# Gated linear attention and a mixture of experts on one core: old state scaled on GpSimd, later weight loads, last tile in one operation, a new order

## The chip, the cores and the metric

The kernel runs on one core of a Trainium2 chip. The metric is the device time of one execution in microseconds (us). The kernel before takes 383.08 us (median of three runs, 382.61 to 383.10).

The engines are named as the profile names them: PE (TensorE matmul) and PEld (its weight loads), DVE (VectorE), ACT (ScalarE), POOL (GpSimd), SP (the engine that issues most DMAs). Each works through its own queue in order.

## The reference

Two parts follow one another. The first is a gated linear attention over 4 batches, 8 heads, 768 tokens and 48 channels per head:

```python
for t in range(S):
    state = alpha[:, :, t, :, None] * state + np.einsum('bhd,bhe->bhde', k[:, :, t], v[:, :, t])
    y[:, :, t] = np.einsum('bhd,bhde->bhe', q[:, :, t], state)
```

Its output, 3072 tokens of 384 channels, goes into a mixture of 8 experts. Each token takes its own best expert, or, where its local gate is at 0.5 or more, the expert of the token before it in its batch. The output row is `p[e] * (relu(x @ w1[e]) @ w2[e])` with hidden size 1024, and `p` the softmax of the 8 logits.

## The kernel before, in words

**Attention.** The tokens are cut into 24 blocks of 128 tokens. Block i belongs to batch i % 4, so the states of four batches (tiles `st`) are carried side by side. A block's inputs come in by three DMAs into one of four slots `x0` to `x3` (slot i % 4): k, q (112x512 each) and the gates a (112x521). The values come by two more DMAs (`vt`, three buffers).

A block goes through these steps. ACT writes a separator into the gates (`mid`, "ACT x<-P 112x4"). DVE scans the gates backwards in two halves into `sf` and forwards into `A`. POOL multiplies k by `sf` and q by `A` in place ("x<-x,sf", "x<-x,A"). PE transposes k ("cs,x 112x112") and multiplies k with q in 64x64 pieces ("x 64x64"). DVE masks that product into `pq`. PE multiplies `pq` with `vt`, and the transposed keys `kk` with `vt`, which updates the state on DVE. PE then adds q times the state ("st,x") to the block's output. ACT copies the output to `XR`, SP stores it to `xd` in DRAM, PE transposes it ("cs,XR") and multiplies it with the gate weights (`logits`).

**The old state.** From the fifth block on, `carry` (line 549) scales the state that the batch had before (part 2 of `s3`) by the total decay of the block, column 0 of each head pair's stretch in `sf`, into part 0 of `s3`. Four ACT operations of 112x48 do it, one for each head pair.

**Routing and experts.** After blocks 8, 16, 20 and 24, `route` finds each token's expert and its place in that expert's list. One expert (number 0) is worked on in two parts, 0a for the first 256 tokens of its list and 0b for the rest. The 0a part starts while the last groups are still being routed. Experts are matmuls in three passes: each weight and each activation is split into a high and a low half (`w1h`, `w1l`, `w2h`, `w2l`, `xh`, `xl`, `hh`). The high half is a cast on ACT; the low half is a subtraction, on POOL for w1 and on DVE for w2. Expert 0's weights come in seven pieces (three of w1 with 512 KB, four of w2 with 384 KB) through four `raw` buffers; the blocks behind whose mask (`marks`) each piece is loaded stand in `WAT`. An output tile is scaled by the token's probability from PSUM into `yo` and scattered to DRAM by an indirect DMA on POOL. The last tile of all (96 rows) is scaled in two halves, one on DVE and one on ACT (lines 1145 to 1150).

**The order.** Nothing is issued where it stands in the code. `add` hands every step to a planner as a task with an engine, a cost, a priority (mostly the block number plus an offset), and what it reads and writes. `Plan.order` runs through the tasks with these costs, takes on each engine the ready task of lowest priority, and writes the queues out in that order. `SHIFT` moves the priority of a kind of task, by engine and by the name that it writes; `ROUTE` and `DUE` move the routing and the early expert; `SLACK`, `TAIL`, `PAGE_US` are the planner's costs of a hand-over, of a DMA's landing and of fetching PE instructions. Where the plan leaves PE idle for a while before the experts start, it puts in filler matmuls ("P<-dz 128x240", results unused); `MARG`, `WINDOW` and `SHARE` decide where and how many. Twenty fillers stand at the start in any case (`WARM`).

## Time and profile before

| | us |
|---|---|
| median of three runs | 383.08 (382.61 to 383.10) |
| profiled execution, its own time | 382.43 |
| its span, first to last instruction | 380.5 |
| PE busy in the span | 367.9 (97%) |
| DVE, ACT, POOL busy in the span | 224.7, 199.3, 203.2 |
| granted TensorE clock, mean | 0.998 |

The page divides the span into 40 slices and gives for each engine the share that it was busy, for PE also the clock that was granted. Busy times of PE are modelled for pipelined matmuls, so that one instruction's end lies behind the start of the next. Fillers count as PE work. In the answers, "idle before" is the time that an engine stood still ahead of a group, with what ended it behind the arrow. 1.93 us of the execution's 382.43 us lie outside the span.

### The profile page before, as it was taken

The numbers are of one execution on the slowest core, as the hardware profiler recorded it, in microseconds if no ns is written. First come the engines' busy times: TensorE is split into PE (matmuls) and PEld (weight loads), VectorE is DVE, ScalarE is ACT, GpSimd is POOL, SyncE is SP. The second block draws the span as 40 slices with busy tenths as digits, with TensorE's granted clock in tenths as the row PEclk, the third lists the DMA queues.
The fourth block names the chain that finished last, engine by engine and source line by source line (L and its number), as shares of the span: only waits on it lengthen the run. The fifth ranks groups of instructions, "written<-read, shape, count | busy, mean of one in ns | idle before, by whom it ended". The sixth has DMA issues, their size and how long they took to land. (4 is left out here: it accounts for less than half of the span.)

```text
span 380.5 us, 10980 instructions
## 1 busy us (share of the span) xinstructions
PE 367.9 (97%) x4151; PEld 342.2 (90%) x4151; DVE 224.7 (59%) x554; ACT 199.3 (52%) x576; POOL 203.2 (53%) x293
## 2 busy tenths in 40 slices
PE   7999999999899999999999999999999999999993
PEld 7988888888788898998899999999999899999993
DVE  5998969878896486455516434642761763543310
ACT  2397687799596573646505523541660672532300
POOL 7765375787547047888624832842663574432012
PEclk9999999999999999999999999999999999999999
DMA  8999999989972255557425622741652552421000
GB/s 217 254 265 262 270 254 258 280 239 261 269 218 75 66 208 161 184 157 249 144 79 180 202 70 65 245 132 43 215 158 83 177 193 62 136 84 43 17 22 28
DMA packets 28665, 62.08 MB, mean 163 GB/s; under 512 B 4660, under 2 KB 11023, under 8 KB 28611
## 3 DMA queue, kind: packets, MB, share of 16 engines
q1 hardware_dynamic: 24576, 51.23, 45.9%
q0 software_dynamic: 3488, 9.86, 7.9%
q8 instruction: 33, 0.54, 0.6%
q10 hardware_dynamic: 546, 0.28, 0.3%
q14 instruction: 22, 0.17, 0.2%
HBM read 51.91 MB, written 9.86 MB: 162 GB/s over the span
## 5 line engine op out<-in xcount | busy, mean ns | idle before, releaser
L329 PE MATMUL P<-w2h,hh_mp 128*128 128x384 f32 (+3 forms) x376 | 100.0, 340 | 0.0
L329 POOL TENSOR_TENSOR w1l<-raw,w1h 128x256 fp32r<-128x256 f32 x96 | 69.6, 750 | 27.9 <-ACT w1h L329 21.0
L329 POOL DMA_INDIRECT out<-yo_mp,li_mp x25 | 26.6, 1063 | 88.8 <-DVE yo_mp L329 71.5
L329 ACT CAST w2h<-raw 128x384 fp32r<-128x384 f32 x64 | 30.8, 512 | 72.6 <-PE P L329 68.6
L329 PEld LDWEIGHTS P<-w2h,hh_mp 128*128 128x128 f32 (+3 forms) x376 | 67.1, 184 | 1.6
L329 PE MATMUL P<-w2l,hh_mp 128*128 128x384 f32 (+4 forms) x200 | 67.4, 337 | 0.0
L329 PE MATMUL P<-xh_mp,w1h 128*128 128x448 f32 (+5 forms) x168 | 59.0, 351 | 0.0
L329 PE MATMUL P<-xl_mp,w1h 128*128 128x448 f32 (+5 forms) x168 | 58.8, 350 | 0.0
L329 PE MATMUL P<-xh_mp,w1l 128*128 128x448 f32 (+5 forms) x168 | 58.8, 350 | 0.0
L329 DVE SCALAR_TENSOR_TENSOR hh_mp<-P,hh_mp 128x384 fp32r<-128x384 f32 (+3 forms) x80 | 34.4, 455 | 41.2 <-ACT hh_mp L329 40.9
L329 DVE TENSOR_SCALAR yo_mp<-P,lw_mp 128x384 f32<-128x384 f32 (+3 forms) x22 | 13.4, 608 | 65.9 <-PE P L329 65.9
L329 ACT ACTIVATE hh_mp<-P 128x448 fp32r<-128x448 f32 (+5 forms) x56 | 29.0, 517 | 38.0 <-PE P L329 36.8
L329 DVE TENSOR_TENSOR w2l<-raw,w2h 128x384 fp32r<-128x384 f32 x64 | 38.8, 638 | 4.7 <-ACT w2h L329 4.0
L329 ACT CAST w1h<-raw 128x256 fp32r<-128x256 f32 x96 | 36.0, 408 | 2.1 <-PE P L329 1.2
L329 POOL TENSOR_TENSOR x<-x,sf 112x512 f32<-112x512 f32 x24 | 28.7, 1198 | 13.9 <-DVE sf L329 6.2
L329 PEld LDWEIGHTS P<-w2l,hh_mp 128*128 128x128 f32 (+4 forms) x200 | 35.5, 177 | 0.5
L329 DVE TENSOR_TENSOR_SCAN sf<-x,P 112x260 f32<-112x260 f32 x48 | 31.2, 680 | 6.6 <-ACT x L329 5.0
L329 ACT COPY XR<-P 64x192 f32<-64x192 f32 x96 | 30.1, 313 | 8.7 <-PE P L329 7.6
L329 POOL TENSOR_TENSOR x<-x,A 112x512 f32<-112x512 f32 x24 | 28.4, 1186 | 10.4 <-DMA x<-akq 4.4
L329 PEld LDWEIGHTS P<-xh_mp,w1h 128*128 128x128 f32 x168 | 31.5, 188 | 1.7
L329 PEld LDWEIGHTS P<-xh_mp,w1l 128*128 128x128 f32 x168 | 31.5, 188 | 1.6
L329 PEld LDWEIGHTS P<-xl_mp,w1h 128*128 128x128 f32 x168 | 31.5, 188 | 1.5
(163 smaller groups left out, 664.0 us busy)
## 6 DMA issues: line engine op xcount, KB each, us to landing
raw<-w SPq DMA_DIRECT2D x24, 512.0 KB, 4.4
raw<-w SPq DMA_DIRECT2D x32, 384.0 KB, 3.4
x<-akq SPq DMA_DIRECT2D x48, 224.0 KB, 5.1
x<-akq SPq DMA_DIRECT2D x24, 227.9 KB, 4.8
vt<-vn SPq DMA_DIRECT2D x48, 96.0 KB, 5.0
xd<-XR SPq DMA_DIRECT2D x24, 192.0 KB, 3.9
xg_mp<-xd,li_mp POOLq DMA_INDIRECT x25, 3.6
out<-yo_mp,li_mp POOLq DMA_INDIRECT x25, 2.7
```

The lines of the kernel that those rows point to most:

```text
L329: r = f(*a, **k)
```

## The change

Four things change. `carry` becomes one POOL operation of 112x192 in which the decay is broadcast along the channels. `WAT` moves expert 0's seven weight pieces from behind blocks 6, 9, 12, 16, 17, 18, 19 to behind 9, 12, 15, 17, 18, 19, 20. The two halves of the last tile go, so that it takes the path of all others, one DVE operation. And the planner's numbers are others: `MARG`, `ROUTE`, `SLACK`, `TAIL`, `DUE`, `SHARE`, `PAGE_US` and the whole table `SHIFT`.

```diff
-MARG = -0.283342
-WAT = (6, 9, 12, 16, 17, 18, 19)
+MARG = -0.12394
+WAT = (9, 12, 15, 17, 18, 19, 20)
...
-ROUTE = (50.6574, -9.18615, 68.2408, 46.086)
-SLACK, TAIL, DUE = 0.0431479, 1.28925, 111.288
+ROUTE = (45.2049, -15.6553, 79.9985, 51.8634)
+SLACK, TAIL, DUE = 0.00592551, 0.771969, 111.747
...
-    "SP k": -1.658, "SP q": -0.77, "SP reg": -0.642, "SP v": -0.878, "SP xd": 3.224,
+    "SP q": 0.345, "SP v": 0.514, "SP xd": -0.986,
...
-WINDOW, SHARE = 3.4, 0.859128
-PAGE, PAGE_AT, PAGE_US, QUEUE = 256, 193, 4.90859, 64
+WINDOW, SHARE = 3.4, 0.939038
+PAGE, PAGE_AT, PAGE_US, QUEUE = 256, 193, 4.12651, 64
...
-        def f():
-            for hp in range(HP):
-                z = hp * 2 * (C + 1)
-                s_.activation(s3[:, 0, hp], s3[:, 2, hp], AF.Copy, scale=SF[:, z:z + 1])
-        add("ACT", 0.95, f, i - 0.75, reads=[kf + (0,), kf + (1,), ("S2", b)], writes=[("S0", b)])
+        add("POOL", 0.58, lambda: g_.tensor_tensor(s3[:, 0], s3[:, 2], SF[:, 0:SW:2 * (C + 1)].unsqueeze(2).broadcast_to(
+            [R, HP, D]), ALU.mult), i - 0.75, reads=[kf + (0,), kf + (1,), ("S2", b)], writes=[("S0", b)], port=True)
...
-                elif self.r == E - 1 and s == len(self.tiles) - 1:
-                    w = DM // 2
-                    add("DVE", 0.4, lambda nm=nm, m=m, s=s, yo=yo: v_.tensor_scalar_mul(
-                        yo()[0:m, w:], ps(nm)[0:m, w:DM], lw()[0:m, s, 0:1]), self.p - 5, reads=[nm, self.wk], writes=[yk + (1,)])
-                    add("ACT", 0.35, lambda nm=nm, m=m, s=s, yo=yo: s_.mul(
-                        yo()[0:m, 0:w], ps(nm)[0:m, 0:w], lw()[0:m, s, 0:1]), self.p - 5, reads=[nm, self.wk], writes=[yk])
```

How the queues move is seen at four places. A row names the operation, what it writes and reads, and its shape; numbers behind a name tell buffers apart, and xN counts equal rows in a stretch.

The first is the start of SP's queue, the loads of the first blocks (112x512 is k or q, 112x521 the gates a). Before:

```order
L329 DMA x0_100<-akq 112x512
L329 DMA x0_100<-akq 112x521
L329 DMA x0_100<-akq 112x512
L329 DMA x1_101<-akq 112x512
L329 DMA x1_101<-akq 112x521
L329 DMA x1_101<-akq 112x512
```

and now:

```order
L329 DMA x0_100<-akq 112x512 x2
L329 DMA x0_100<-akq 112x521
L329 DMA x1_101<-akq 112x512 x2
L329 DMA x1_101<-akq 112x521
L329 DMA x2_102<-akq 112x512 x2
L329 DMA x2_102<-akq 112x521
```

The gates of block 0, which the first scans read, were the second load and are the third.

The second is the start of DVE's queue. Before:

```order
L329 MEMSET zz 128x256
L329 MEMSET P 112x260
L329 CAST dz<-zz 128x256
L329 MEMSET P 112x2
L329 SCALAR_TENSOR_TENSOR iota<-one 128x128
L329 MEMSET zz 128x128
```

and now:

```order
L329 MEMSET zz 128x256
L329 MEMSET P 112x260
L329 SCALAR_TENSOR_TENSOR iota<-one 128x128
L329 MEMSET P 112x2
L329 MEMSET zz 128x128
L329 CAST dz<-zz 128x256
```

The cast that makes the fillers' operand `dz` has gone behind the scan that makes `iota` and two memsets.

The third is POOL's queue at blocks 4 to 7 (slots 0 to 3). Before:

```order
L329 TENSOR_TENSOR x0_100<-x0_100,sf0_107 112x512
L329 TENSOR_TENSOR x0_100<-x0_100,A0_109 112x512
L329 TENSOR_TENSOR x1_101<-x1_101,sf1_108 112x512
L329 TENSOR_TENSOR x2_102<-x2_102,sf0_107 112x512
L329 TENSOR_TENSOR x1_101<-x1_101,A1_110 112x512
```

and now:

```order
L329 TENSOR_TENSOR x0_100<-x0_100,sf0_107 112x512
L329 TENSOR_TENSOR st0_123<-st0_123,sf0_107 112x192
L329 TENSOR_TENSOR x0_100<-x0_100,A0_109 112x512
L329 TENSOR_TENSOR x1_101<-x1_101,sf1_108 112x512
L329 TENSOR_TENSOR st1_124<-st1_124,sf1_108 112x192
L329 TENSOR_TENSOR x2_102<-x2_102,sf0_107 112x512
L329 TENSOR_TENSOR x1_101<-x1_101,A1_110 112x512
```

The scaling of the old state stands between a block's "x<-x,sf" and its "x<-x,A", or between those of two blocks.

The fourth is PE's queue at blocks 14 and 15 (slots 2 and 3, `vt2` and `vt0`). Before:

```order
L329 MATMUL P_99<-cs_72,XR1_116 128x128 x3
L329 MATMUL P_99<-st2_125,x2_102 64x48 x16
L329 MATMUL P_99<-x3_103 64x64 x16
L329 MATMUL P_99<-dz_127 128x240 x11
L329 MATMUL P_99<-vt0_104,pq1_114 64x96 x8
```

and now:

```order
L329 MATMUL P_99<-st1_124,x1_101 64x48 x16
L329 MATMUL P_99<-x2_102 64x64 x16
L329 MATMUL P_99<-x3_103 64x64 x16
L329 MATMUL P_99<-cs_72,x0_100 128x112 x4
L329 MATMUL P_99<-cs_72,XR1_116 128x128 x3
L329 MATMUL P_99<-oi_162,one_86 128x72
L329 MATMUL P_99<-oh0_76,trif_87 128x8x8
L329 MATMUL P_99<-vt2_106,pq0_113 64x96 x8
```

Eleven fillers stood between block 15's key-query product and the product with its mask; now that product is issued a block earlier, and other work follows it. Over the whole queue PE has the same matmuls as before but for the fillers. There were 106, in runs of 51, 5, 7 and 2 (to block 2), 10, 9, 4 and 11 (blocks 8 to 15) and 7 (before the experts). There are 90, in runs of 48, 10, 6 and 6 (to block 2), 6 (block 4), 5 (between blocks 17 and 18) and 4 and 5 (before the experts).

## Rows read from the trace of the kernel before

**Rows 1.** Stretches (us): busy time of each engine, clock, DMA share, GB/s.

```profile
core 0: us, PE busy (x) PEld busy (x) DVE busy (x) ACT busy (x) POOL busy (x), PEclk, DMA share, GB/s
1.90:10.00 8.10, 8.03 (x51) 8.04 (x52) 4.49 (x15) 2.36 (x6) 6.28 (x54) 1.00 1.03 269
20.00:118.00 98.00, 94.74 (x2171) 81.45 (x2167) 84.86 (x193) 80.34 (x272) 62.13 (x73) 1.00 0.88 249
20.00:131.20 111.20, 107.45 (x2458) 92.61 (x2453) 92.04 (x217) 87.76 (x294) 65.10 (x75) 1.00 0.81 230
131.20:374.50 243.30, 242.39 (x1431) 232.61 (x1427) 117.10 (x306) 104.73 (x264) 122.72 (x151) 1.00 0.41 130
```

**Rows 2.** Timeline, the fillers on PE: start, duration, engine, what, count.

```profile
36.27 1.39 PE L329 MATMUL P<-dz 128*128 128x240 f32 x10
...
55.79 1.25 PE L329 MATMUL P<-dz 128*128 128x240 f32 x9
...
60.59 0.70 PE L329 MATMUL P<-dz 128*128 128x240 f32 x4
...
82.05 1.50 PE L329 MATMUL P<-dz 128*128 128x240 f32 x11
```

**Rows 3.** Waits of POOL and of DVE from 20 to 118 us.

```profile
POOL x L329 <- DMA x<-akq: 7.7, 8, 1.8
...
DVE sf L329 <- ACT x L329: 3.6, 3, 1.9
```

**Rows 4.** Timeline, the start of the span, all engines.

```profile
1.36 0.55 DVE L329 CAST dz<-zz 128x256 fp32r<-128x256 f32 x1
1.84 0.41 DVE L329 TENSOR_TENSOR_SCAN iota<-one 128x128 f32<-128x128 f32 x1
...
1.97 8.26 PE L329 MATMUL P<-dz 128*128 128x240 f32 x51 [1.97 <-DVE dz L329]
2.23 0.17 DVE L329 MEMSET zz<- 128x128 f32 x1
...
5.99 0.18 ACT L329 ACTIVATE x<-P 112x4 f32<-112x4 f32 x1 [0.21 <-DMA x<-akq]
...
7.56 1.19 POOL L329 TENSOR_TENSOR x<-x,sf 112x512 f32<-112x512 f32 x1 [0.80 <-DVE sf L329]
...
10.07 0.55 PE L329 MATMUL P<-cs,x 112*128 112x112 f32 x4
```

**Rows 5.** Groups by shape: busy us, mean ns, idle before and its releasers.

```profile
L329 ACT ACTIVATE st<-st,sf 112x48 f32<-112x48 f32 x80 | 20.2, 323 | 1.2 <-DVE sf L329 0.9
...
L329 POOL TENSOR_TENSOR w1l<-raw,w1h 128x256 fp32r<-128x256 f32 x96 | 69.6, 750 | 27.9 <-ACT w1h L329 21.0 <-PE P L329 4.0 <-ACT x L329 2.4
...
L329 POOL TENSOR_TENSOR w<-hhh,PL 128x96 f32<-128x96 f32 x2 | 0.7, 356 | 0.1
```

**Rows 6.** Timeline, scaled queries on POOL and their products on PE, two blocks.

```profile
24.69 1.19 POOL L329 TENSOR_TENSOR x<-x,A 112x512 f32<-112x512 f32 x1 [1.80 <-DMA x<-akq]
...
25.93 0.69 PE L329 MATMUL P<-x 48*64 48x64 f32 x32 [0.24 <-POOL x L329]
...
82.34 1.19 POOL L329 TENSOR_TENSOR x<-x,A 112x512 f32<-112x512 f32 x1
...
85.58 0.69 PE L329 MATMUL P<-x 48*64 48x64 f32 x32
```

**Rows 7.** Operations on the w2 halves, 90 to 125 us: ns min/median/max.

```profile
L329 DVE TENSOR_TENSOR w2l<-raw,w2h x8: 542/592/1468, 99.8 to 119.0; 128x384 fp32r<-128x384 f32 x8
```

**Rows 8.** Timeline, the end of the span: DVE, ACT, POOL.

```profile
370.35 0.62 DVE L329 TENSOR_SCALAR yo_mp<-P,lw_mp 128x384 f32<-128x384 f32 x1 [3.60 <-PE P L329]
...
371.24 0.99 POOL L329 DMA_INDIRECT out<-yo_mp,li_mp  x1 [3.22 <-DVE yo_mp L329]
...
374.54 0.41 DVE L329 TENSOR_SCALAR yo_mp<-P,lw_mp 96x192 f32<-96x192 f32 x1 [3.57 <-PE P L329]
374.99 0.42 ACT L329 ACTIVATE yo_mp<-P,lw_mp 96x192 f32<-96x192 f32 x1 [12.54 <-DVE yo_mp L329]
...
375.68 0.92 POOL L329 DMA_INDIRECT out<-yo_mp,li_mp  x1 [3.44 <-ACT yo_mp L329]
```

More of the change, by code (lines that the diff above doesn't have):

```diff
@@ L47 @@
 ZW = SW // 2
-MARG = -0.283342
-WAT = (6, 9, 12, 16, 17, 18, 19)
+MARG = -0.12394
+WAT = (9, 12, 15, 17, 18, 19, 20)
 WARM = 20
-ROUTE = (50.6574, -9.18615, 68.2408, 46.086)
-SLACK, TAIL, DUE = 0.0431479, 1.28925, 111.288
+ROUTE = (45.2049, -15.6553, 79.9985, 51.8634)
+SLACK, TAIL, DUE = 0.00592551, 0.771969, 111.747
 SHIFT = {
-    "ACT PL": -0.127, "ACT RA": 8.623, "ACT S": 0.908, "ACT XR": 2.762, "ACT a": 3.543, "ACT cm": -2.661, "ACT cs": 4.785,
-    "ACT ex": 0.905, "ACT kk": -1.035, "ACT km": 0.644, "ACT lc": -2.008, "ACT oh": 2.104, "ACT ol": 0.705, "ACT olx": -5.091,
-    "ACT xx": -0.221, "ACT z": 1.649, "DVE A": 17.221, "DVE LA": 1.576, "DVE Lk": 5.254, "DVE PL": -0.575, "DVE S": -0.809,
-    "DVE a": -6.486, "DVE cm": 2.124, "DVE cst": 0.933, "DVE desc": -2.158, "DVE dz": -3.077, "DVE em": -3.387,
-    "DVE eq": -0.046, "DVE ex": 10.665, "DVE g": 2.457, "DVE ge": 2.364, "DVE hs": 1.855, "DVE iota": 0.612, "DVE kr": 0.686,
-    "DVE ky": 0.563, "DVE lo": -0.039, "DVE lt": -3.229, "DVE m": -1.173, "DVE oi": -5.497, "DVE pn": 2.409, "DVE po": -1.438,
-    "DVE pq": 1.809, "DVE ps": 0.385, "DVE sel": 0.789, "DVE seli": -1.667, "DVE sf": 1.456, "DVE t": -5.473, "DVE z": 0.436,
-    "PE kp": 2.487, "PE lg": 33.407, "PE lp": 0.275, "PE lt": -0.799, "PE pe": 19.271, "PE pw": 4.648, "PE rb": 0.955,
-    "PE rp": -8.707, "PE up": 9.175, "PE wu": -2.797, "PE xp": 0.85, "PE y": -2.763, "POOL LA": 6.286, "POOL cst": 6.067,
-    "POOL hh": -2.562, "POOL ipt": -2.109, "POOL k": -10.562, "POOL oh": 5.115, "POOL one": -3.299, "POOL q": 2.065,
-    "POOL rrr": 1.814, "POOL thr": 2.424, "POOL trif": 0.605, "POOL vz": -7.632, "POOL w": 1.042, "SP a": -1.131,
-    "SP k": -1.658, "SP q": -0.77, "SP reg": -0.642, "SP v": -0.878, "SP xd": 3.224,
-}
@@ L67 @@
-WINDOW, SHARE = 3.4, 0.859128
-PAGE, PAGE_AT, PAGE_US, QUEUE = 256, 193, 4.90859, 64
+    "ACT PL": -0.361, "ACT RA": -2.485, "ACT XR": -1.989, "ACT cm": 0.356, "ACT cs": 0.121, "ACT ex": -0.311,
+    "ACT kk": -1.259, "ACT km": 1.631, "ACT lc": 7.876, "ACT oh": -0.026, "ACT ol": -1.015, "ACT olx": -7.987,
+    "ACT wgs": -2.496, "ACT xd": 1.735, "ACT xx": 1.521, "ACT z": -3.748, "DVE A": 0.709, "DVE Lk": -0.194, "DVE PL": -0.715,
+    "DVE S": 1.495, "DVE Z": -1.371, "DVE a": 7.714, "DVE cm": -0.736, "DVE cst": 0.44, "DVE desc": 0.018, "DVE dz": 3.959,
@@ new lines @@
+    "DVE em": -0.173, "DVE eq": -3.276, "DVE ge": 0.41, "DVE hs": -3.08, "DVE iota": -3.599, "DVE kr": 22.354,
+    "DVE ky": -1.212, "DVE lo": 0.785, "DVE lt": 0.79, "DVE m": -0.109, "DVE mx": -1.405, "DVE oi": 0.628, "DVE pn": -0.347,
+    "DVE po": 3.16, "DVE pq": 1.893, "DVE ps": -0.096, "DVE rr": 2.094, "DVE se": 2.327, "DVE sel": 0.279, "DVE self": 1.051,
+    "DVE seli": 1.107, "DVE sf": 8.472, "DVE t": -3.049, "DVE z": -1.088, "PE kp": 9.173, "PE lg": -0.796, "PE lp": 0.131,
+    "PE lt": 0.73, "PE pw": -3.122, "PE rb": -0.144, "PE rp": -2.066, "PE up": -5.335, "PE wu": 0.377, "PE xp": 3.853,
@@ L69 @@
+    "POOL LA": 3.271, "POOL S": 1.826, "POOL cst": 1.579, "POOL k": -0.119, "POOL oh": -0.025, "POOL one": -0.487,
+    "POOL q": 0.843, "POOL rrr": 0.277, "POOL thr": 0.072, "POOL vz": 0.378, "POOL w": 6.292, "SP a": 0.636, "SP k": 0.039,
+    "SP q": 0.345, "SP v": 0.514, "SP xd": -0.986,
+}
+WINDOW, SHARE = 3.4, 0.939038
+PAGE, PAGE_AT, PAGE_US, QUEUE = 256, 193, 4.12651, 64
 NX, NV, NA, NR, NK = 4, 3, 2, 3, 5
```

## The prediction

> **What bounds the kernel now.** I read the busy times by stretch first [rows 1]. From 131.2 us on, where the experts run, PE is busy for 242.39 of 243.30 us, and the change gives PE the same matmuls in nearly the same order there. That stretch I take as fixed. What can move is the end of the attention, that is, the time at which the expert matmuls begin, and the few microseconds behind the last matmul.
>
> In the attention PE looks as full, 107.45 of 111.20 us from 20 us on [rows 1], but this figure holds fillers. Next I read the fillers on PE's timeline: four runs with 34 fillers in the middle of the attention, together 1.39 + 1.25 + 0.70 + 1.50 = 4.84 us, or 0.14 us each [rows 2]. Where the planner put a filler, PE had nothing useful to do. So 4.84 us of fillers and 111.20 - 107.45 = 3.75 us of plain idleness are what PE could win there.
>
> Then I asked who makes PE wait. No single engine is full: of 98 us DVE works 84.86, ACT 80.34, POOL 62.13, and the DMA engines 88% [rows 1]. The waits agree: POOL waits 7.7 us for loads of k and q, DVE 3.6 us for ACT's separators [rows 3]. The attention is thus a pipeline of several nearly full engines with a good order, and PE last in line. Moving work off one engine helps only as far as the next lets it.
>
> **The change part by part.** The sum is made against the profiled execution (382.43 us, span 380.5); the median of the runs is 0.65 us above it, and the forecast is the median plus the sum.
>
> *Last tile.* The halves were meant to run side by side, but ACT's starts at 374.99, just when DVE's (374.54, 0.41 long) is over; POOL's scatter follows at 375.68, 1.14 us after DVE began. The tile before it, done in one operation, took 0.62 us and its scatter began 371.24 - 370.35 = 0.89 us after DVE began [rows 8]. The last tile in one operation should do the same: 0.25 us less, on the path that sets the end. Bounds: 0, if something else holds the scatter, and -0.4, if the hand-over to POOL is shorter. I take -0.25.
>
> *Opening.* Three things. The cast of `dz` now waits behind the scan for `iota` (0.41 us) and two memsets (0.17 us for the long one), so the first filler comes some 0.6 us later than 1.97 [rows 4]. The fillers up to block 2 go from 51 + 5 + 7 + 2 to 48 + 10 + 6 + 6: three fewer at first (-0.4 us at 0.14 each), eight more after that (+1.1). PE would thus be 0.6 - 0.4 + 1.1 = 1.3 us later. The other side is the data. The gates of block 0 are now the third load. ACT's separator waits for them at 5.99 us [rows 4], and one load of 112x512 floats is 229 KB, 0.85 us at the 269 GB/s of that stretch [rows 1], so scans and scaling come 0.85 us later. The first transposes had room for this: their operand was ready at 7.56 + 1.19 = 8.75 us, and PE came out of its fillers only at about 10.0 [rows 4]. The two delays run side by side; I take +1.0, bounds -0.4 (only the shorter first run counts, later slack takes the rest) and +1.3.
>
> *Middle.* The 34 fillers go, and 6 (block 4) and 5 (block 17) come, 1.6 us: gross -3.3. But a filler only covers a wait; if the new order does not remove the wait, it comes back as plain idleness. What speaks for real removal: ACT loses 80 operations of 323 ns [rows 5], 20 us of 80; its separators are then in time for DVE, which waited 3.6 us for them. And the three w1 pieces come nine loads of k, q and a later, so that the loads of blocks 11 to 20 stand behind one piece less, 524 KB or about 2 us, where POOL waited 7.7 us for loads in all [rows 3]. Against: the planner now counts a DMA's landing 0.5 us shorter and a hand-over 0.04 us shorter, and the chip's did not change, so the order is tighter than before; and DVE, at 87% of its stretch, gets nothing off. I let 1.0 of the 3.3 us come back: -2.3, bounds -5.0 (also half of the 3.75 us idle goes) and 0 (all comes back).
>
> *The old state on POOL.* Twenty operations of 112x192. No row shows one: 128x96 takes 356 ns and 128x256 takes 750 ns [rows 5], so each costs between these, and on the line between them 0.59 us; 20 are 12 us (7 to 15). POOL has 98 - 62.13 = 36 us free in the stretch, which hides them in sum. In place they stand before a block's scaled queries. Two rows show the cover: in one block PE waited right at the end of that scaling (25.88, PE at 25.93), in another it took up the product 2.05 us after it (83.53 and 85.58) [rows 6]. I cost it at 0 in the sum. If the cover is gone in a block, it is up to 0.59 us there (a rival below).
>
> The Trainium skill, "GPSIMD Engine Reference", section "3.1 Elementwise — side-by-side cycle accounting", gives 4497 ns for a two-input operation of 2048 floats. That would be an estimated 0.42 us for 192 and 8 us for the twenty, and the sum stays the same.
>
> *Later weights, end of the attention.* The last w2 piece now comes behind all loads of k and q. Its casts end before the second matmuls of part 0a, which start only some 11 us after the first: 0, with a lower end of -1.5 us (a rival below). Before the experts 4 + 5 fillers stand for 7: +0.3, bounds 0 and +0.3.
>
> Sum: -0.25 + 1.0 - 2.3 + 0.3 = -1.25 us. The profiled execution would take 381.2, the median 381.8.
>
> **Rivals.** *The loads set the pace.* If the DMA engines and not the order bound the attention, the opening costs nothing, since the bytes are the same, and the last q loads come one w2 piece (393 KB, 1.5 us at 269 GB/s) earlier: -1.5 - 0.25, 381.3 us. For it: 249 GB/s over 98 us against 269 in the opening [rows 1]. Against: 12% of the DMA time is free, and PE's plain idleness is small.
>
> *The waits come back in part.* If only about a third of the 3.3 us is won, -1.1 + 1.0 + 0.3 - 0.25 leaves 383.0 us, no change. For it: DVE's load; the next engine is never far.
>
> *They come back whole.* PE then pays the opening and wins nothing: +1.0 + 0.3 - 0.25, 384.1 us. The place is DVE's queue, which starts 0.85 us late behind the gates and has 13 us free in 98; the side turns where less than 1.05 of the 3.3 us stays won.
>
> *The old state blocks POOL.* Each operation holds back the scaled queries behind it. If 7 of the 20 blocks have no cover, as the one at 25.93 us, PE loses 7 x 0.59 = 4.1 us: +2.9, 386.0 us. From three such blocks on (1.8 us) the kernel is slower. For it: the row at 25.93. Against: the 2 us of cover at 85.58, and POOL's load of 63%.
>
> The Trainium skill, "SBUF — State Buffer", section "Who interferes with whom", speaks against more work on GpSimd too: a VectorE operation with two inputs from SBUF and a GpSimd operation that reads SBUF exclude each other for a whole instruction. Here the scans, the mask and the state updates take one input from PSUM, and only the eight subtractions for w2's low halves have two from SBUF; the longest of them took 1468 ns against 542 for the shortest [rows 7], which agrees. By that rule the twenty new operations could hold DVE for 8 x 0.59 = 4.7 us at most (386.5 us if all of it were on the path); I give it no more than its part in this rival.
>
> **How the numbers follow.** Forecast 0.45 (own range 380.6 to 382.7), loads 0.15, back in part 0.13, back whole 0.17, POOL blocked 0.10. The time is that of the forecast, 381.8. For eight times in ten the range goes down to 379.8, where the middle wins its lower bound and the opening little, and up to 384.9, which takes in the case in which all comes back and the smaller part of the blocked POOL. A measurement of this kernel can tell about 0.2% from no change, 0.77 us. Faster than 382.3 are most of the forecast (0.36) and of the loads (0.13): 0.49. Within 0.2%: 0.09 + 0.02 + 0.11 + 0.03 = 0.25. Slower: the rest, 0.26.
>
> **What would show it.** In the profile after, the scatter of the last tile should start 0.9 us after DVE takes up the tile. The first transposes should come between 9.7 and 10.5 us, the first expert matmul at about 130.2 instead of 131.2, and from there to the last matmul it should again be 243 us. Fillers between 30 and 120 us should be one run of 5, with plain idleness of PE between 20 us and the experts under 5.5 us; 7 us or more there says that the waits came back. ACT should be busy some 20 us less, POOL 12 us more, and waits of PE for "POOL x" above 2 us would be the blocked POOL. If the experts' stretch itself changes by more than 0.5 us, the argument is wrong from its start.

## The result and the profile after

The changed kernel takes 378.03 us (median of six runs, 376.37 to 381.44); the kernel before took 383.09 us in the same comparison. The ratio is 0.9865 (95% interval 0.9822 to 0.9908), 5.06 us less. Forecast were 381.8 us in a range of 379.8 to 384.9: the direction was right, the size was not. The profiled execution took 376.37 us, the lowest of the six, with a span of 374.5 us against 380.5. The two profiles thus lie 6.1 us apart (382.43 and 376.37), 1.0 us more than the medians.

The experiments ran on several chips, and on some of them the granted clock was lower in many whole runs (0.971 to 0.999, and on one chip the kernel before took 385.3 us at 0.995 or more and 391.7 at 0.985), so that an experiment is compared by its ratio to the kernel before on its own chip, and where the interval does not decide, the median of the runs with a mean clock of 0.995 or more stands beside it ("at equal clock").

The stretches of the kernel after, in the columns of [rows 1]; 126.17 us is where the experts begin now:

```profile
core 0: us, PE busy (x) PEld busy (x) DVE busy (x) ACT busy (x) POOL busy (x), PEclk, DMA share, GB/s
1.90:10.00 8.10, 7.59 (x50) 7.49 (x51) 3.67 (x11) 2.21 (x6) 5.54 (x53) 1.00 1.02 269
20.00:118.00 98.00, 95.17 (x2290) 83.70 (x2289) 87.42 (x203) 64.76 (x200) 75.71 (x95) 1.00 0.89 253
20.00:126.17 106.17, 103.26 (x2450) 90.73 (x2448) 91.15 (x218) 69.81 (x216) 75.71 (x95) 1.00 0.84 239
126.17:368.20 242.03, 242.03 (x1430) 232.63 (x1427) 115.28 (x306) 104.20 (x264) 123.16 (x151) 1.00 0.41 131
```

In the 98 us from 20 on, ACT falls from 80.34 to 64.76 us and POOL rises from 62.13 to 75.71. PE, which lost nothing but fillers, and DVE, which lost nothing, are busier than before (95.17 against 94.74 and 87.42 against 84.86): more of the same work falls into these 98 us. The experts begin at 126.17 instead of 131.20 us, 5.03 us earlier. From there PE no longer stands still once.

The fillers of the kernel after from 20 us on, on PE's timeline (start, duration, engine, what, count):

```profile
25.30 0.92 PE L329 MATMUL P<-dz 128*128 128x240 f32 x6
...
90.16 0.81 PE L329 MATMUL P<-dz 128*128 128x240 f32 x5
...
123.28 0.69 PE L329 MATMUL P<-dz 128*128 128x240 f32 x4
...
124.30 0.80 PE L329 MATMUL P<-dz 128*128 128x240 f32 x5
```

Together they are 3.22 us. Before there were 4.84 us [rows 2] and one more run of 7 just ahead of the experts, 1.03 us. That gives the account of PE from 20 us to the experts:

| us | before | after | difference |
|---|---|---|---|
| fillers | 5.87 | 3.22 | -2.65 |
| idle, as the views show it | 3.75 | 2.91 | -0.84 |
| the rest, matmuls with work | 101.58 | 100.04 | -1.54 |
| length | 111.20 | 106.17 | -5.03 |

The second line is not the change's doing. It holds waits of PE for which the profile shows no releaser (it calls them issue), here before and after, up to the experts:

```profile
PE P L329 <- issue: 1.2, 3, 0.5
```

```profile
PE P L329 <- issue: 0.2, 1, 0.2
```

In the two other profiles of the changed kernel (`after_again` and `after_control`, below) they are 1.3 and 1.0 us, and the first expert matmul comes at 127.17 and 126.47 us. Without them PE's idleness is the same before and after (2.6 and 2.7 us), and about 1.0 of the 5.03 us is such a difference between profiles.

The third line falls although PE has 0.9 us more of this work left at 20 us than before (the opening, below; counted without fillers, 12 matmuls more). We read this as stalls inside the stretches in which PE counts as busy: the end of a pipelined matmul is modelled, and a short wait between two groups can vanish under it. That is inferred from the account and not measured by itself. What a view shows of it is that the waits of the weight loads (PEld) in these stretches sum to 8.6 us instead of 10.3, and some of these are idleness of PE as well.

Where along the attention the gain arises is sought in the starts of the logits, one group for every four blocks, read from PE's timeline of each kernel. The last two lines count the matmuls, without fillers, that start ahead of each group:

| start, us | first transposes | logits of blocks 0-3 | 4-7 | 8-11 | 12-15 | 16-19 | 20-23 | first expert matmul |
|---|---|---|---|---|---|---|---|---|
| before | 10.07 | 32.37 | 51.54 | 71.59 | 92.39 | 116.03 | 130.41 | 131.20 |
| after | 9.78 | 33.34 | 50.70 | 66.64 | 87.98 | 111.89 | 125.32 | 126.17 |
| matmuls ahead, before | | 488 | 924 | 1366 | 1840 | 2304 | 2594 | |
| matmuls ahead, after | | 484 | 920 | 1294 | 1804 | 2288 | 2594 | |

The kernel after is 1.0 us late at the first group, 0.8 early at the second and 5.0 early at the third. But the new order has the third group ahead of 72 matmuls that came before it in the old one; at the mean of 0.042 us (101.58 us for 2417) these are an estimated 3 us. So some 2 us are won there, some 3 at the fourth group (36 matmuls), and the full 5 only at the last, where the counts agree: the gain grows along the attention and does not come at one place. The waits that stood in [rows 3] from 20 to 118 us are these now (total, times, longest):

```profile
POOL x L329 <- DMA vt<-vn: 1.6, 1, 1.6
...
DVE sf L329 <- ACT x L329: 0.5, 2, 0.3
```

GpSimd waits once for a transfer instead of eight times (1.6 us, 7.7 before), and DVE almost never for ACT's separators (0.5 us, 3.6 before).

The start of the span, which answers to [rows 4]:

```profile
1.89 0.47 DVE L329 CAST dz<-zz 128x256 fp32r<-128x256 f32 x1
...
2.41 7.47 PE L329 MATMUL P<-dz 128*128 128x240 f32 x48 [2.41 <-DVE dz L329]
...
6.96 0.18 ACT L329 ACTIVATE x<-P 112x4 f32<-112x4 f32 x1 [0.28 <-DMA x<-akq]
...
8.54 1.19 POOL L329 TENSOR_TENSOR x<-x,sf 112x512 f32<-112x512 f32 x1 [1.78 <-DVE sf L329]
...
9.78 0.60 PE L329 MATMUL P<-cs,x 112*128 112x112 f32 x4
```

The separator is 0.97 us later than before (6.96 against 5.99) and the scaled keys are ready at 9.73, just when the first transposes begin. Groups by shape, answering to [rows 5] (busy us, mean ns, idle before with its releasers):

```profile
L329 POOL TENSOR_TENSOR x<-x,A 112x512 f32<-112x512 f32 x24 | 30.1, 1261 | 1.7 <-DVE A L329 1.3 <-PE P L329 0.4
...
L329 POOL TENSOR_TENSOR st<-st,sf 112x192 f32<-112x192 f32 x20 | 10.2, 513 | 8.8 <-PE P L329 4.6 <-DVE sf L329 3.6 <-DVE x L329 0.4
```

The new operation takes 513 ns. The end of the span, answering to [rows 8]:

```profile
368.53 0.61 DVE L329 TENSOR_SCALAR yo_mp<-P,lw_mp 96x384 f32<-96x384 f32 x1 [3.57 <-PE P L329]
369.42 0.92 POOL L329 DMA_INDIRECT out<-yo_mp,li_mp  x1 [3.20 <-DVE yo_mp L329]
```

The last scatter starts 0.89 us after DVE takes the tile. Last, one row of the kernel before that [rows 1] holds within its 0.91 us of idleness among the experts, and that has no counterpart after:

```profile
152.28 0.40 PE L329 MATMUL P<-cs,xg_m 64*128 64x64 f32 x3 [0.85 <-DMA xg_m<-xd,li_m]
```

Part 0b's gather came too late for PE there. The way from the first expert matmul to the end of the span is 1.0 us shorter (249.3 and 248.3), and all of it lies ahead of the last tile: from the first expert matmul to DVE's start on that tile it is 243.3 us before and 242.4 after, and the 0.91 us of idleness that are gone are nearly all of the difference. The 0.25 us of the last tile do not show at the end of this pair: from the start of its scatter to the end of the span it is 4.86 us before and 5.11 after. This last part lies between 4.86 and 5.22 us in all profiles of these runs, whichever form the tile has. Taken over all of them the 0.25 us are there: from DVE's start to the end of the span it is 6.0 to 6.4 us in the six profiles with two halves, and 5.8 to 6.1 in the fourteen with one operation.

### The profile page after: what moved, and what is told of

It is laid out like the page before. It is cut to its first block, busy times and chain, and to the rows that moved or that the text cites. A ratio compares the mean times of both kernels' runs of the same rounds, so it can differ in the third digit from the quotient of the medians.

```text
span 374.5 us, 10866 instructions
## 1 busy us (share of the span) xinstructions
PE 363.0 (97%) x4135; PEld 339.7 (91%) x4135; DVE 221.2 (59%) x554; ACT 179.6 (48%) x495; POOL 213.7 (57%) x313
## 4 chain that ended last, share of the span: by engine, by line
PE 79%; DVE 6%; ACT 2%; issue 1%; DMA 1%; POOL 0%; POOLq 0%; DVEq 0%; ACTq 0%
PE P L329 79%; DVE sf L329 2%; DVE A L329 2%; ACT XR L329 1%; DMA xd<-XR 1%; DVE pq L329 1%; DVE st L329 1%; DVE P L329 0%; ACT ol L329 0%; POOL out L329 0%; DVE yo_mp L329 0%; ACT x L329 0%; DVE em L329 0%; POOLq L1247 0%; ACT xx L329 0%
## 5 line engine op out<-in xcount | busy, mean ns | idle before, releaser
L329 DVE TENSOR_SCALAR yo_mp<-P,lw_mp 128x384 f32<-128x384 f32 (+2 forms) x22 | 13.6, 618 | 64.5 <-PE P L329 64.5
L329 DVE TENSOR_TENSOR w2l<-raw,w2h 128x384 fp32r<-128x384 f32 x64 | 36.5, 605 | 3.6 <-ACT w2h L329 3.1
L329 POOL TENSOR_TENSOR x<-x,A 112x512 f32<-112x512 f32 x24 | 30.1, 1261 | 1.7 <-DVE A L329 1.3
```

Of the source, the lines that this page charges most:

```text
L329: r = f(*a, **k)
```

## The experiments

Three theories stood against each other. *Order*: the new queues make the gain by themselves. *ACT*: its 20 us held the attention up, and any order wins when they go. *Loads*: the early w1 pieces held up k, q and a.

### Edits without the numbers, numbers without the edits

Here the planner orders the work anew. In `edits_old_numbers` the kernel before gets the three edits and keeps its numbers:

```diff
-WAT = (6, 9, 12, 16, 17, 18, 19)
+WAT = (9, 12, 15, 17, 18, 19, 20)
...
-        add("ACT", 0.95, f, i - 0.75, reads=[kf + (0,), kf + (1,), ("S2", b)], writes=[("S0", b)])
+        add("POOL", 0.58, lambda: g_.tensor_tensor(s3[:, 0], s3[:, 2], SF[:, 0:SW:2 * (C + 1)].unsqueeze(2).broadcast_to(
...
-                elif self.r == E - 1 and s == len(self.tiles) - 1:
...
```

> The kernel before with the three edits (old state on GpSimd, later weight loads, last tile in one operation) but with all planner numbers of before; the planner orders the work anew for the changed tasks. If the edits themselves make the gain (ACT relieved by 20 us, w1 loads later), it comes near the changed kernel: 378.5 to 380 us, first expert matmul at 126 to 128 us. If the new numbers, that is the order, make it: 382 to 384 us, first expert matmul at 130 to 132 us.

Measured: ratio 0.9919 (0.9876 to 0.9961), at equal clock 383.9 us (7 runs) against 385.3 (7 runs); first expert matmul 129.46 us, which here stands ahead of the last logits (132.58) and so does not mark the end of the attention. The edits alone win about 1.4 us, between the two expectations. `numbers_no_edits` is the same diff the other way round, made in the changed kernel.

> The changed kernel's planner numbers, with the old state on ACT in four operations, weights behind the blocks of before, and the last tile in two halves. If the order makes the gain: 378.5 to 380 us. If the edits make it: 382 to 384.5 us, with DVE waiting 3 us or more for ACT's separators and POOL 6 us or more for loads between 20 and 118 us.

Measured: 1.0056 (1.0012 to 1.0100), first expert matmul 133.20 us. The numbers alone lose. Of the waits that were expected without the edits, GpSimd's for loads is there (6.3 us) and DVE's for the separators is not (0.9). Neither theory alone is left: 1.4 us won and about 2 us lost do not add up to 5 us won.

### The square of order and edits

A new plan moves everything. So in the next six kernels the order is kept to the instruction, and only the edit itself moves. For the old state, the task keeps its engine and place in the plan, and only what it issues is changed, here in the order of before:

```diff
         def f():
-            for hp in range(HP):
-                z = hp * 2 * (C + 1)
-                s_.activation(s3[:, 0, hp], s3[:, 2, hp], AF.Copy, scale=SF[:, z:z + 1])
+            g_.tensor_tensor(s3[:, 0], s3[:, 2], SF[:, 0:SW:2 * (C + 1)].unsqueeze(2).broadcast_to([R, HP, D]), ALU.mult)
         add("ACT", 0.95, f, i - 0.75, reads=[kf + (0,), kf + (1,), ("S2", b)], writes=[("S0", b)])
```

For the weights, load, casts and low halves of the three w1 pieces are moved in the finished order by the time between two masks:

```diff
+MOVES, WARM = ((0, 6, 9), (1, 9, 12), (2, 12, 15)), 20
...
+def moved(plan, out):
+    by = {n: plan.marks[b].start - plan.marks[a].start for n, a, b in MOVES}
+    return [(a + by.get(getattr(t, "piece", None), 0.0), i, t) for a, i, t in out]
```

The last tile is left out of this: it has two halves in all kernels in the order of before and is one operation in all in the order of after, 0.25 us of the difference between the two columns below.

In the order of before:

> The order of before kept to the instruction on PE, DVE and SP; only the four ACT operations of the old state are replaced by one on GpSimd at the same place in the program. Theory that ACT's 20 us held the attention up: DVE's wait for ACT's separators (3.6 us) goes and 1 to 3 us are won, 380 to 382 us. Theory of the order: what PE waits for is set by the queues, 382.5 to 383.5 us. If the operation delays the scaled queries on GpSimd: 384 us or more.

> The order of before, with only expert 0's three w1 pieces (load, casts, low halves) moved from behind blocks 6, 9, 12 to behind 9, 12, 15. Theory that these loads held up k, q and a: GpSimd's wait for loads (7.7 us between 20 and 118 us) falls below 4 us and 1 to 3 us are won, 380 to 382 us. Theory of the order: 382.5 to 383.5 us, since the fixed queues wait elsewhere.

> The order of before with both edits at once (old state in one GpSimd operation, the three w1 pieces behind blocks 9, 12, 15), every other instruction where it stood. Theory that the new order turns the freed time into earlier work and the old one cannot: 382 to 384.5 us, no gain, GpSimd again waiting over 10 us for the operands of the state's operation. Theory that the two edits only work together, whatever the order: 379.5 us or less.

In the order of after each edit is taken back in the same way, the state by the four ACT operations in the place of GpSimd's one, the weights by this line:

```diff
+MOVES, WARM = ((0, 9, 6), (1, 12, 9), (2, 15, 12)), 20
```

> The changed kernel's order kept to the instruction on PE, DVE and SP; only the old state goes back to ACT, four operations at the place of the one on GpSimd. Theory that the new order lives on ACT's free time: 2 to 5 us more than the changed kernel, 380 to 383 us, with DVE or PE waiting for ACT again. Theory that the order alone makes the gain, whoever scales the state: within 1 us of the changed kernel.

> The changed kernel's order, with only expert 0's three w1 pieces (load, casts, low halves) moved from behind blocks 9, 12, 15 to behind 6, 9, 12, as before. Theory that these loads held k, q and a up: GpSimd's wait for loads rises from 1.6 to 4 us or more between 20 and 118 us and the time by 1 to 3 us. Theory of the order, or of ACT: within 1 us of the changed kernel.

> The changed kernel's order with both edits taken back at once: the old state in four ACT operations, the three w1 pieces behind blocks 6, 9, 12. With the kernels before it fills the square of order and edits. Theory that order and edits pay only together: 2 us or more slower than the kernel before, ratio 1.005 to 1.015. Theory that the order has a worth of its own: ratio 0.998 or less.

The changed kernel itself, unaltered, ran twice more, once beside the first two of these three and once beside the last runs on the opening:

> The changed kernel once more, beside the runs below on the same chip, as the measure for them. If its gain is the same on every chip: 0.983 to 0.990 of the kernel before. If part of its first gain came from single longer runs of the kernel before, in which the granted clock fell: compared at equal clock 4.5 to 5.5 us less, with a ratio that depends on how often the clock falls in either.

> The changed kernel unaltered, as the measure for the three beside it on this chip. 0.980 to 0.990 of the kernel before, 4 to 6 us less at equal granted clock.

Ratios to the kernel before on the same chip, with their intervals:

| old state on, w1 pieces behind | order of before | order of after |
|---|---|---|
| ACT, 6, 9, 12 | 1 | 1.0053 (1.0018 to 1.0089) |
| ACT, 9, 12, 15 | 1.0038 (0.9990 to 1.0086) | 1.0052 (1.0025 to 1.0079) |
| GpSimd, 6, 9, 12 | 0.9985 (0.9930 to 1.0040) | 0.9890 (0.9849 to 0.9930) |
| GpSimd, 9, 12, 15 | 0.9934 (0.9891 to 0.9977) | 0.9865, 0.9876, 0.9857 |

The last cell in the order of before (both edits) looks like a small gain, but at equal clock it is 384.8 us (5 runs) against 385.2 (2 runs), and its first expert matmul comes at 132.49 us: no gain that the trace shows.

So the old state on GpSimd is worth little in the order of before: nothing that can be told with the early w1 pieces (at equal clock 385.3 us in 3 runs against 385.3 in 7), and 1.0% with the late ones (at equal clock 384.8 us in 5 runs against 386.8 in 3, on different chips). In the order of after it is worth 1.6% with the early pieces and 1.8% with the late ones (there 384.92 against 377.98 us on one chip, 6.9 us; 2 to 5 were expected by the theory that the order lives on ACT's free time). And the new order without it is half a per cent slower than before. Most of the gain belongs to the two together.

The w1 pieces decide less. In the old order the late ones win nothing, though GpSimd's wait "POOL x <- DMA x<-akq" falls from 7.7 to 4.1 us. In the new order the early ones take 379.5 us at equal clock (6 runs) against 378.0 (6 runs), some 1.5 us, but the intervals of the ratios overlap, and of the 2.7 us by which the first expert matmul comes later there (129.88 against 127.17 on that chip) 1.1 stand already at the first transposes (10.71 and 9.61) and 1.0 are issue waits. The wait behind it came back as the theory of the loads has it: "POOL x <- DMA x<-akq" 4.8 us in 6 times.

Why the old order wins little is seen in the waits of `before_plan_carry_pool`, from 20 to 118 us, first GpSimd's and then ACT's:

```profile
POOL st L329 <- DVE sf L329: 10.6, 6, 4.2
POOL st L329 <- PE P L329: 6.7, 5, 2.7
```

```profile
ACT kk L329 <- PE P L329: 9.0, 9, 2.1
ACT xx L329 <- PE P L329: 8.8, 10, 2.1
ACT XR L329 <- PE P L329: 7.6, 9, 1.9
```

and ACT's in the kernel before:

```profile
ACT XR L329 <- PE P L329: 4.4, 5, 1.3
...
ACT kk L329 <- PE P L329: 2.0, 3, 1.5
...
ACT xx L329 <- PE P L329: 0.7, 2, 0.5
```

At ACT's old place the state's operation reaches the head of GpSimd's queue before its operands are there, and GpSimd stands 17.3 us in front of it. ACT, 20 us freer, waits for PE 25.4 us instead of 7.1: the freed time became waiting, since the next copies in its queue have nothing to copy yet. DVE's wait for the separators, which the prediction had counted on, did fall (from 3.6 to 1.0 us), and it made no difference.

One rival is not excluded by the square: the operation stands at ACT's old place there, and part of what is called the order may be this one place in GpSimd's queue. Against it speaks `edits_old_numbers`, where the planner gave the operation a place of its own under the old numbers and all three edits won only 1.4 us. The old queues with this operation alone at another place were not run.

In the new order the reverse holds. The waits of PE in `after_plan_carry_act`, from 20 us to its experts at 134.02:

```profile
PE P L329 <- ACT kk L329: 2.3, 3, 1.1
PE P L329 <- ACT xx L329: 1.7, 3, 0.7
PE P L329 <- ACT lc L329: 1.3, 1, 1.3
```

With the 80 operations back, ACT is late for PE with the transposed keys, the transposed outputs and the logits. In the kernel after none of these three waits is there; PE waits 1.3 us for XR and 1.0 us for all else. It is the time of the four operations and not their place in ACT's queue that makes ACT late: ACT never stands idle ahead of one of them there. We read this as follows: the new order has placed other ACT work close to where PE needs it, and that holds only while ACT is free.

### Are fillers only covers?

`before_plan_no_fillers` leaves out the 34 fillers of [rows 2]:

```diff
+        done += getattr(t, "key", "") == "PE kp"
+        if isinstance(t, tuple) and 4 <= done < NB:
+            continue
```

> The kernel before without its 34 fillers in blocks 8 to 15 (4.84 us), all other instructions in the same order. Theory that fillers only cover waits: the time stays within 1 us of before, the first expert matmul within 0.7 us, and the fillers' places show idle time of PE instead. Theory that fillers themselves delay the matmuls behind them: 2 us or more are won. If the clock needs them: it falls between 36 and 90 us and the kernel is 2 us or more slower.

Measured: 0.9986 (0.9958 to 1.0014), first expert matmul at 131.14 us against 131.20. The stretch up to there, and PE's first waits in it:

```profile
20.00:131.14 111.14, 103.83 (x2431) 88.78 (x2427) 93.06 (x217) 87.74 (x294) 65.33 (x75) 1.00 0.81 231
```

```profile
PE P L329 <- DVE st L329: 2.2, 5, 0.9
PE P L329 <- DVE pq L329: 1.7, 3, 1.3
...
PE P L329 <- POOL x L329: 1.3, 2, 0.8
```

PE's idleness rises from 3.75 to 7.31 us, while the first expert matmul stays where it was and the granted clock at 1.00: a filler that goes is replaced by the wait under it. The waits under the fillers of before were for DVE and GpSimd. So the 2.65 us of fillers that the change removes were won because the waits went.

### Is the old state's operation hidden?

`after_plan_carry_twice` issues it twice in the order of after; `carry_twice_again` is the same kernel beside the changed one.

```diff
+            g_.tensor_tensor(s3[:, 0], s3[:, 2], SF[:, 0:SW:2 * (C + 1)].unsqueeze(2).broadcast_to([R, HP, D]), ALU.mult)
             g_.tensor_tensor(s3[:, 0], s3[:, 2], SF[:, 0:SW:2 * (C + 1)].unsqueeze(2).broadcast_to([R, HP, D]), ALU.mult)
```

> The changed kernel with each of the 20 GpSimd operations on the old state issued twice (the second writes the same values again), everything else in the same order. Theory that they lie beside other work, as the prediction costed them (0): within 0.8 us of the changed kernel. If GpSimd's queue is on the path in a third of the blocks: 3 to 4 us more. Rival, GpSimd holding DVE: DVE's scans and state updates get longer and the time rises by 2 us or more.

> Once more the changed kernel with every GpSimd operation on the old state issued twice, now beside the changed kernel on one chip. Theory that they lie beside other work: within 0.8 us of it. Theory that in the new order GpSimd is close to the path: 1.5 to 4 us more, to be seen at the logits of block 8 and later.

Measured: 0.9817 (0.9779 to 0.9855) on one chip, and 0.9894 (0.9842 to 0.9946) on another, beside 0.9857 (0.9805 to 0.9909) of the changed kernel. One lies below and one above, so no cost can be told. The groups of `carry_twice_again`, the first over the whole span, the other two from 20 to 118 us:

```profile
L329 POOL TENSOR_TENSOR st<-st,sf 112x192 f32<-112x192 f32 x40 | 20.6, 516 | 5.4 <-PE P L329 1.6 <-DVE sf L329 1.1 <-DVE pq L329 1.0
```

```profile
L329 DVE TENSOR_TENSOR_SCAN sf<-x,P 112x260 f32<-112x260 f32 x40 | 26.0, 678 | 1.0 <-POOL x L329 0.3 <-DMA vt<-vn 0.3 <-ACT x L329 0.2
L329 DVE TENSOR_TENSOR_SCAN A<-x,P 112x520 f32<-112x520 f32 x21 | 25.6, 1225 | 1.4 <-POOL x L329 1.0
```

The 10.3 us added replace waits of GpSimd (its idleness ahead of the operation falls from 8.8 to 5.4 us). The first expert matmul is 1.5 us later than in the changed kernel on that chip (127.95 and 126.47), of which 0.75 stand already at the first transposes (10.56 and 9.81), ahead of any of these operations, and 0.9 are more issue waits (1.9 and 1.0 us from 20 us on): nothing is left for the operations. The profile of `after_plan_carry_twice` itself can't tell: its first expert matmul comes at 130.41 us, with 4.5 us of issue waits ahead of it. DVE's scans keep their 678 and 1225 ns (678 and 1223 after): GpSimd doesn't hold them up.

### The opening

`after_gates_first` loads the gates of blocks 0 to 3 ahead of k and q, and cuts the first fillers to 36:

```diff
-        out.sort(key=lambda x: (x[0], x[1]))
+        out = sorted(((a if isinstance(t, tuple) or t not in GATES else GATES[t].start - 0.01, i, t) for a, i, t in out), key=lambda x: (x[0], x[1]))
...
-            for _ in range(t[2]):
+            for _ in range(t[2] - (cut.pop() if cut else 0)):
```

> The changed kernel with the gates of blocks 0 to 3 loaded ahead of k and q of their block (they were third), and the first run of fillers cut from 48 to 36. Theory that the opening is a chain from the first gates through DVE and GpSimd to PE: ACT's separator comes at about 5.1 us instead of 6.96, the first transposes at about 7.9 instead of 9.8, and 1.0 to 1.9 us of it are kept to the end: 376 to 377 us. Rival, the loads or DVE set the pace later on and the gain is lost by block 8: 377.5 to 378.5 us.

Measured: 0.9787 (0.9732 to 0.9843), lower than the changed kernel's ratios, but without that kernel on the chip; the trace shows no gain (first logits at 33.76 us against 33.34). The separator came at 7.08 us, not at 5.1: ahead of it in ACT's queue stood two operations that write `PL`, and they waited for constants. `after_gates_first_clear` moves these two and a DVE copy of a constant behind the first blocks:

```diff
+        late = [next(t for t in self.tasks if t.key == k) for k in ("ACT PL", "DVE desc")]
+        out = [(a + 16.0 * (t in late), i, t) for a, i, t in out]
```

> As the kernel with the gates first (and 36 fillers at the start), but ACT's two operations that write PL and DVE's copy of a constant, which stood ahead of the first separator and the first scan in their queues and waited for the constants, now stand behind the first blocks. Theory that these two held the opening once the gates came early: the first separator at 5.0 to 5.5 us instead of 7.0, the first transposes at 7.8 to 8.3, the first expert matmul 1 us or more earlier than in the changed kernel, and 1 us less in all. Rival, later blocks wait for loads or for DVE anyway: the first transposes come early, and by the logits of block 8 (50.5 us) nothing is left of it.

The start of its span:

```profile
2.41 6.83 PE L331 MATMUL P<-dz 128*128 128x240 f32 x36 [2.41 <-DVE dz L331]
...
4.62 0.18 ACT L331 ACTIVATE x<-P 112x4 f32<-112x4 f32 x1 [1.26 <-DMA x<-akq]
...
6.83 1.18 POOL L331 TENSOR_TENSOR x<-x,sf 112x512 f32<-112x512 f32 x1
...
9.08 0.55 PE L331 MATMUL P<-cs,x 112*128 112x112 f32 x4
...
16.10 0.55 PE L331 MATMUL P<-cs,x 112*128 112x112 f32 x4
```

The separator is 2.3 us earlier and the scaled keys are ready at 8.01, but the 36 fillers take 6.83 us, so that the first transposes come only 0.7 us earlier; block 2's are 0.1 us earlier than in the changed kernel on the same chip (16.10 and 16.18), and the logits of blocks 4 to 7 start at 50.38 against 50.22. From 80 us on this profile can't be compared: PE has an issue wait of 2.2 us, and the granted clock is 0.83 between 80 and 100 us. The rival was right, and sooner than it said. Ratio 0.9835 (0.9769 to 0.9900) beside 0.9857; at equal clock 381.1 us (3 runs) against 379.9 (2 runs). This version does not beat the changed kernel.

The other side of the opening is PE's. `after_first_fillers_only` drops all fillers but the first 48; `first_fillers_only_again` is the same kernel beside the changed one.

```diff
+        seen += isinstance(t, tuple)
+        if isinstance(t, tuple) and seen > 1:
+            continue
```

> The changed kernel without any filler but the first 48: the runs of 10, 6, 6, 6, 5, 4 and 5 are gone, all other instructions in the same order. Theory that fillers only cover waits: within 0.6 us of the changed kernel, with the waits seen as idle time of PE. If the eight added fillers of the opening delay PE, as the prediction costed them: 0.9 to 1.3 us less. If the clock falls without them: 2 us or more above.

> Once more the changed kernel without any filler but the first 48, now beside the changed kernel on one chip. Theory that fillers only cover waits: within 0.6 us of it, the second block's transposes at 12.9 us as there. If the added fillers of the opening delay PE: the block 2 transposes at 15.6 instead of 16.5 us, and 0.9 us less at the end.

Measured: 0.9852 (0.9817 to 0.9887) and 0.9889 (0.9845 to 0.9934), the second beside 0.9857: no difference that can be told. Block 2's transposes come at 15.71 instead of 16.18 us, so the fillers did delay PE by half a microsecond there, but the first logits start at 32.90 against 32.86. What PE gains in the first three blocks is gone after four. Further on the profiles without fillers are behind: the first expert matmul comes at 129.12 and 130.01 us against 126.47, with 3.7 and 2.8 us of issue waits ahead of it against 1.0. Whether the missing fillers have a part in these waits stays open.

### The last tile

`before_last_tile` takes only the two halves out of the kernel before.

```diff
-                elif self.r == E - 1 and s == len(self.tiles) - 1:
-                    w = DM // 2
...
```

> The kernel before with the last tile in one DVE operation, nothing else. By the prediction 0.25 us less: the last scatter starts 0.9 us after DVE takes the tile instead of 1.14. That is less than the comparison of times can tell, and is read in the profile. Rival: something else holds the scatter, and it starts 1.1 us or more after it.

Measured: 1.0049 (1.0008 to 1.0090). None of its twelve runs had a mean clock of 0.995 or more, so a quarter of a microsecond can't be read from the times. Its profile:

```profile
380.33 0.61 DVE L329 TENSOR_SCALAR yo_mp<-P,lw_mp 96x384 f32<-96x384 f32 x1 [3.57 <-PE P L329]
381.22 0.93 POOL L329 DMA_INDIRECT out<-yo_mp,li_mp  x1 [3.20 <-DVE yo_mp L329]
```

0.89 us from DVE's start to the scatter, as in the kernel after and as forecast.

## Why the prediction came out too small

**Last tile, -0.25.** Right in its step: 0.89 instead of 1.14 us, in every kernel with one operation. At the end of the profiled span it did not show, since what follows the scatter took 0.25 us longer there; over all profiles it does.

**Opening, +1.0.** The size was right at its place: block 2's transposes start at 16.46 instead of 15.54 us (+0.92) and the first logits at +0.97; in the two other profiles of the changed kernel block 2's are at 16.30 and 16.18. Both causes that were named are there, the gates (0.97 us later) and the fillers (0.5 us of PE's delay). But neither is on the path: the gates loaded first, or the fillers left out, win nothing from the first group of logits on. What makes the new order 1.0 us late at the first group stays open.

**Middle, -2.3, with the fillers ahead of the experts -2.0.** This is the step that failed: "I let 1.0 of the 3.3 us come back". From block 2's transposes (+0.92) to the first expert matmul (-5.03) 5.95 us were won in this pair of profiles. About 1.0 of it is issue waits, which differ from profile to profile; without them it is 4.9, and 5.1 and 4.8 in the two other profiles of the changed kernel, where 2.0 were forecast. Of that, 2.65 us are fillers, near the 3.0 that were counted with those ahead of the experts: nothing of them came back. The plain idleness, of which the lower bound let half go, did not fall (2.6 and 2.7 us without the issue waits). The other 2.5 (1.54 of the account, and the 0.92 of work that PE was behind at 20 us) went out of the stretches in which PE counts as busy, and the sum had them at nothing: it took fillers and plain idleness for all that PE could win, though busy time of pipelined matmuls is modelled. That these 2.5 us are short stalls is inferred, and which waits they were stays open; that they went only where edit and order came together is what the square shows.

**The range.** Its lower end does not follow from the prediction's own terms. With the middle at its lower bound of -5.0, the last tile at -0.25, the fillers ahead of the experts at +0.3 and the opening at 0, the sum gives 378.1 us, and with the opening at its full +1.0 it gives 379.1; neither is 379.8. The measured 378.03 lies beside the first.

Behind the failed step stands a wrong picture of the coupling. "Moving work off one engine helps only as far as the next lets it" was meant as a reason for a small gain. The square shows a harder form of it: ACT's 20 us are worth between nothing and 2 us in the old queues and 6.9 us in the new ones. The forecast added the parts as if each had a price; here the price of the largest edit is set by the order around it. The argument that the new planner costs, tighter than before, would bring waits back was not borne out: with 21 fillers fewer from 20 us on, PE's idleness stayed the same without the issue waits.

**The old state on POOL, 0.** Right in sum: 10.2 us more on GpSimd, no wait of PE for GpSimd's scaled queries, and twice as many of them cost nothing that a trace shows, while the times can't tell. The estimate of 0.59 us an operation lay above the measured 0.51. By the Trainium skill, "GPSIMD Engine Reference", section "3.1 Elementwise — side-by-side cycle accounting", it was estimated at 0.42; the trace lies between the two.

**Later weights, 0.** Right: among the experts PE does not stand still at all, so none of them came too late.

**The experts, fixed.** Wrong by 0.9 us, more than the 0.5 that the prediction allowed itself. One wait of PE for the gather of part 0b (0.85 us at 152.28) is gone. In the kernel before it was counted in the 0.91 us of idleness of that stretch and not looked at.

**The rivals.** "The loads set the pace" may have a part in it: the w1 pieces made some 1.5 us in the new order, which is not clear of the noise, and GpSimd's waits for k, q and a are gone. "The waits come back", in part or whole, did not happen here, but it is what happens when the edit is made without the order. "The old state blocks POOL" is likewise what GpSimd shows in the order of before (17.3 us of waiting), there without costing the kernel time. Of the signs that were foretold, the first transposes at 9.78, one run of five fillers between 30 and 120 us, idleness under 5.5 us and ACT 20 us freer (179.6 us busy in the span against 199.3) all came as foretold, while the first expert matmul came at 126.17 instead of 130.2.

## What to carry to other kernels

When the queues are in a fixed order, time freed on an engine is not a gain but an offer: in the old order it turned into waits of ACT and GpSimd for operands, and only queues written for it took it up. So an edit and an order that were made together are to be valued together; undoing the edit within the new order (6.9 us) and making it within the old one (0 to 2) are two cheap experiments that tell which it is. And PE's reserve can be more than fillers and idleness: here 2.5 of the 4.9 us that the attention won came out of time in which PE counted as busy. Last, a difference of 1 us between two single profiles can be waits that neither kernel is the cause of: several profiles of one kernel show how large these are.

## What the runs showed of the hardware

**GpSimd held by DVE.** In the kernel after, one "x<-x,A" took 3037 ns where the others take 1185 (minimum, median and maximum by tile, and the timeline around it):

```profile
L329 POOL TENSOR_TENSOR x<-x,A x24: 1172/1185/3037, 10.0 to 110.1; 112x512 f32<-112x512 f32 x24
```

```profile
108.96 4.18 POOL L329 TENSOR_TENSOR x<-x,A 112x512 f32<-112x512 f32 x2
...
110.15 1.95 DVE L329 TENSOR_TENSOR w2l<-raw,w2h 128x384 fp32r<-128x384 f32 x4
112.70 0.85 DVE L329 TENSOR_TENSOR w2l<-raw,w2h 128x384 fp32r<-128x384 f32 x1 [0.60 <-ACT w2h L329]
```

DVE does four subtractions back to back with both inputs in SBUF, 1.95 us in all, and the GpSimd operation that starts beside them, the second of the two, is 1.85 us longer. A fifth subtraction starts while it still runs (it ends at 113.14) and takes 0.85 us, where the four took 0.55 each. The prediction looked at the other direction, GpSimd holding DVE. The Trainium skill, "SBUF — State Buffer", section "Who interferes with whom", says that a VectorE operation with two inputs from SBUF contends with a GpSimd operation that reads SBUF. The trace agrees, and here it is GpSimd that is held, for nearly the length of all four.

**A pause of PE, and its clock behind it.** In the profile of `numbers_no_edits` PE waited 3.04 us for something that the profile doesn't show (it calls it issue), ahead of part 0b's first matmul. The stretches around it, in the columns of [rows 1]:

```profile
155.40:158.40 3.00, 0.03 (x1) 0.00 (x0) 0.00 (x0) 0.30 (x1) 2.19 (x3) 1.00 0.88 296
158.40:159.40 1.00, 0.89 (x6) 0.72 (x6) 0.36 (x1) 0.02 (x1) 0.00 (x0) 1.00 0.42 85
159.40:161.00 1.60, 1.60 (x10) 1.60 (x9) 0.84 (x3) 0.45 (x2) 0.52 (x1) 0.52 0.20 80
161.00:162.70 1.70, 1.70 (x10) 1.70 (x9) 0.20 (x3) 1.03 (x3) 1.67 (x3) 0.50 0.32 116
162.70:166.00 3.30, 3.30 (x31) 3.30 (x30) 1.26 (x6) 2.08 (x8) 2.60 (x4) 0.97 0.22 60
```

The granted clock goes to 0.50, 1.2 GHz, about 1 us after the pause, and PE does 20 matmuls in 3.3 us; back at 2.4 GHz it does 31 in the same time. At that pace 20 would have taken 2.1 us, so the pause of 3 us costs an estimated 1.2 us more. Waits of this kind differ from profile to profile: the changed kernel had 0.2, 1.3 and 2.8 us of them in its three profiles, and the experiments up to 6.4. What PE waits for there was not settled.
